# A decode step with grouped attention: VectorE's program as a loop, and the folding of the V groups moved to TensorE

## The chip, the core and the metric

One core of a Trainium2 chip runs the whole program. Its engines are TensorE (PE in the profile, its weight loads PEld), VectorE (DVE), ScalarE (ACT), GpSimd (POOL) and SyncE (SP), which here issues nearly all loads. Data comes from HBM into the on-chip SBUF; TensorE writes to PSUM, eight banks of 128 x 512 float32. The metric is the device time of one execution in microseconds (us), as the median of the runs.

## The reference

For a batch of 8 rows with 512 features, one decode step is computed, all in float32:

```python
xn = layernorm(x)
q = (xn @ wq) -> 32 heads of 128;  k, v: cached, 8 heads of 4096 x 128 (4 query heads share one)
scores = q . k * 128 ** -0.5
s = concat(softmax(scores) . v) @ wo
z = gelu(xn @ w_in)                       # 2 x 896
g = silu((z1 * (w_sp * layernorm(z2) + b_sp)) @ w_out)
return x + s * g
```

The caches of k and v hold 2 x 8 x 8 x 4096 x 128 numbers, 268 MB; wq and wo 8.4 MB each; the weights of the MLP 5.5 MB.

## The kernel before, in words

Three slots A, B and C of 8.4 MB in SBUF take every load. For each of the 8 key heads, four loads come in this order: K of batches 0 to 3 into A, K of batches 4 to 7 into B, V of batches 0 to 3 into C, V of batches 4 to 7 into B. At the start wq goes into B and the MLP's weights into C. In the last head V of batches 0 to 3 goes into A, the last V comes in two halves, and wo comes into C in seven pieces (`load_wo`). A load is queued on SP as soon as the last reader of its slot is done; the loads share one queue and are served in order.

TensorE's work for a head: `scores` (L506) multiplies the spread queries `qz` with K, in four column groups, so that the 4096 keys stand as 4 groups of 1024 in `sc`. `softmax` takes the maximum of each group (L510), exponentials (L511), the common maximum and sum over the groups by small transpositions and a product with `same`, a matrix of ones where two partitions belong together; it scales p (L524), turns it by eight transpositions (L528) and copies it to `tbuf` (L529). `values(b)` (L538) multiplies p of one batch with V in four column groups c: 16 rows of each group's 32 partitions of `o_ps` hold group x query row, 4 x 4, by 4 x 128 columns, of which only the blocks on the diagonal (group of the row equal to group of the columns) are wanted. VectorE masks the others away with `diag` (L540) and adds the four column blocks (L541) into `o_sb`. `combine(b)` (L544), issued behind the values of the next batch, then adds the four partition groups with one product of `o_sb` (128 x 128) by `fold` (128 x 4) into `po`. At the end of a head VectorE stores `po` into `oT` (L606), and spreads the next head's queries into `qz` (L499).

wo's products follow in the last head: `folded_wo` (L566) for the heads that are done, placed between and behind the last values, then `direct_wo` (L574) for the last two heads, a product that joins both (L625), and on VectorE the gate (L630) and the residual (L631).

The order is what the program's text gives. A recorder collects all operations with what they read and write and inserts the waits. TensorE runs the first seven heads as a hardware loop (`LOOPED = 7`), whose waits take tokens: the producer adds one, TensorE takes one. The last head and all other engines are written out.

Of the kernel before, what the change touches and what calls it, by code (L numbers as in the profile page):

```python
# [15 lines left out]
P = 128  # L16
# [3 lines left out]
G = 4  # L20
# [59 lines left out]
class Op:  # L80
    def __init__(self, eng, name, args, kw, line):
        self.eng, self.name, self.args, self.kw, self.line = eng, name, args, kw, line
        self.reads, self.writes = [], []
        self.waits = []
        self.sem = None
        self.iter = None
        self.pos = None


class Recorder:  # L90
# [6 lines left out]
    NAMES = ["tensor", "vector", "scalar", "gpsimd", "sync"]  # L97

    def __init__(self, nc):
        self.nc = nc  # L100
        self.ops = []
        self.touched = {}
        self.now = None
        self.rounds = 0
        self.order = {n: [] for n in self.NAMES}
        self.dma_sems = {}
        for n in self.NAMES:
            setattr(self, n, Proxy(self, n))

    @contextmanager  # L110
    def round(self, i):
        self.now = i
        self.rounds = max(self.rounds, i + 1)
        self.count = {n: 0 for n in self.NAMES}
        yield
        self.now = None

    def add(self, eng, name, args, kw):
# [3 lines left out]
        key = kw.pop("key", None)  # L122
# [15 lines left out]
        if self.now is not None:  # L138
            op.iter, op.pos = self.now, self.count[eng]
            self.count[eng] += 1  # L140
        op.at = len(self.order[eng])
# [3 lines left out]
        op.deps = set()  # L145
# [25 lines left out]
    def plan(self):  # L171
# [18 lines left out]
        body = [op for op in self.order["tensor"] if op.iter is not None]  # L190
        size = len(body) // self.rounds
        rounds = [body[i * size:(i + 1) * size] for i in range(self.rounds)]
        place = {(o.eng, o.iter, o.pos): o for o in self.ops if o.iter is not None}
        for p in range(size):
            need = set()
            for i, ops in enumerate(rounds):
                assert ops[p].pos == p and ops[p].name == ops[0 * size + p].name
                for o in ops[p].waits:
                    assert o.iter == i, (ops[p].line, ops[p].name, i, o.eng, o.line, o.iter)
                    need.add((o.eng, o.pos))  # L200
            for i, ops in enumerate(rounds):
                ops[p].waits = [place[e, i, q] for e, q in sorted(need)]
        takes = [o.pos for op in rounds[0] for o in op.waits if not o.dma]
        assert takes == sorted(set(takes)), takes
        assert all(o.dma or o.eng == "vector" for op in rounds[0] for o in op.waits)

        for op in self.ops:
            op.token = op.counted = False
        for op in self.ops:
            for o in op.waits:  # L210
                if o.dma:
                    continue
                if op.eng == "tensor" and op.iter is not None:
                    o.token = True
                else:
                    o.counted = True
        for p in range(size):
            any_ = any(ops[p].counted for ops in rounds)
            for ops in rounds:
                ops[p].counted = any_  # L220

        nc = self.nc
        self.first = None
        self.sems = {}

        def sem(name):
            if name not in self.sems:
                self.sems[name] = nc.alloc_semaphore(name)
            return self.sems[name]

        for n in self.NAMES:
            c = 0
            for op in self.order[n]:
                if op.dma:
                    op.sem = sem(op.key or f"dma{op.n}")
                    op.taken = op.key is not None
                    continue
                if op.token and op.counted:
                    c += 1
                elif op.counted:  # L240
                    c += 1
                op.level = c
            sem(n)
        sem("token")

    def emit_op(self, op):
        nc = self.nc
        eng = getattr(nc, op.eng)
        with nc.source_location(__file__, op.line, op.name):
            waits = []  # L250
            for o in sorted(op.waits, key=lambda o: o.n):
                if o.dma:
# [3 lines left out]
                    else:  # L256
                        waits.append((o.sem, 16))
                elif op.eng == "tensor" and op.iter is not None:
                    t = self.sems["token"]
                    eng.wait_ge(t, 1).then_inc(t, -1)  # L260
                else:
                    waits.append((self.sems[o.eng], o.level))
            for s, v in waits:
# [6 lines left out]
            elif op.counted:  # L270
                ins.then_inc(self.sems[op.eng], 1)
                if op.token:
                    eng.wait_ge(self.sems[op.eng], op.level).then_inc(self.sems["token"], 1)
            elif op.token:
                ins.then_inc(self.sems["token"], 1)

    def emit(self):
        nc = self.nc
        self.plan()
        for n in self.NAMES[1:]:  # L280
            for op in self.order[n]:
                self.emit_op(op)
        ops = self.order["tensor"]
        inside = [i for i, op in enumerate(ops) if op.iter is not None]
        size = len(inside) // self.rounds
        for op in ops[:inside[0]]:
            self.emit_op(op)
        with nc.tensor.Fori(0, self.rounds):
            for op in ops[inside[0]:inside[0] + size]:
                self.emit_op(op)  # L290
        for op in ops[inside[-1] + 1:]:
# [28 lines left out]
def gqa_gmlp_decode(real, x, kT, v, wq, wo, w_mlp, out):  # L320
# [13 lines left out]
    for c in range(0, XW, XW // X_PARTS):  # L334
# [22 lines left out]
    nc.vector.tensor_reduce(same[:, 0, :], ident.rearrange("p (g r) -> p r g", g=G),  # L357
                            op=ALU.add, axis=AX.X)
    for g in range(1, G):
        nc.vector.tensor_copy(same[:, g, :], same[:, 0, :])  # L360
# [5 lines left out]
    nc.vector.tensor_reduce(fold, same[:, 0, :G * REP].rearrange("p (g r) -> p r g", g=G),  # L366
                            op=ALU.add, axis=AX.X)
    same8 = sb("same8", [P, (E - 1) * B + R])
    nc.gpsimd.memset(same8, 0.0)
    nc.vector.tensor_copy(same8[:, (E - 1) * B:E * B], same[:, 0, :B])  # L370
# [8 lines left out]
    o_ps = [psum(f"o_ps{i}", [P, G, DH]) for i in range(2)]  # L379
    po = psum("po", [P, 512])[:, :B * REP]  # L380
    scr = [psum(f"scr{i}", [P, 512]) for i in range(3)]
    for t in o_ps:
        nc.vector.memset(t, 0.0)
# [5 lines left out]
    nc.vector.tensor_scalar(rstd[:, 0:1], mv[:, 1:2], EPS, None, op0=ALU.add)  # L389
# [5 lines left out]
    nc.vector.tensor_copy(xnT[:, :, :B], pt.rearrange("p (k b) -> p k b", k=NK))  # L395

    gate, xg, wb = sb("gate", [P, W]), sb("xg", [P, W]), sb("wb", [P, 2])
# [7 lines left out]
    nc.vector.tensor_copy(xg, px[:, :W])  # L405
    nc.vector.tensor_copy(wb, px[:, W:])
# [3 lines left out]
    def project_q(quad):  # L410
# [9 lines left out]
        tv = tq.rearrange("p (r g c) -> p r g c", r=REP, g=G)  # L420
        for g in range(G):
            h = quad * G + g
            nc.vector.tensor_copy(qT[:, h], tv[:, :, g, :B].rearrange("p r b -> p b r"))

    def mlp():
# [4 lines left out]
        pz = scr[1]  # L430
        nc.vector.memset(pz, 0.0)
# [9 lines left out]
        nc.vector.tensor_copy(zf, pz)  # L441
# [7 lines left out]
        def mean(src, pm, name):  # L449
# [3 lines left out]
            nc.vector.tensor_scalar(t, pm, 1.0 / FH, None, op0=ALU.mult)  # L453
# [6 lines left out]
        nc.vector.memset(u[(G - 1) * R:, 0, FH - (G - 1) * FQ:], 0.0)  # L460
        var = mean(u[:, 0, :], scr[2][:, :1], "var")
        nc.vector.tensor_scalar(var, var, EPS, None, op0=ALU.add)
# [8 lines left out]
        nc.vector.tensor_copy(hT.rearrange("p a s -> p (a s)"), th)  # L471
# [4 lines left out]
        nc.vector.tensor_copy(y_sb, sc[:, 0, :])  # L476
# [13 lines left out]
    nmin, full = sb("nmin", [1, R]), sb("full", [1, G, R])  # L490
    w, wl = sb("w", [P, 1]), sb("wl", [P, 1])
    oT = sb("oT", [P, FOLDED // REP, REP, B])
    o_all = [sb(f"o_all{i}", [P, G, DH]) for i in range(2)]
    o_sb = [sb(f"o_sb{i}", [P, DH]) for i in range(2)]
# [3 lines left out]
    def spread_q(h):  # L498
        nc.vector.tensor_copy(qz.rearrange("p (b s) -> p b s", b=B)[:, :, :REP], qT[:, h])  # L499
# [9 lines left out]
    def softmax():  # L509
        nc.vector.tensor_reduce(nm, sc, op=ALU.max, axis=AX.XY, negate=True)  # L510
        nc.scalar.activation(p.rearrange("p j s -> p (j s)"), sc.rearrange("p c s -> p (c s)"), AF.Exp,  # L511
                             bias=nm, accum_out=l)
        a, mm, tot = scr[0][:1, :P], scr[1][:, :1], scr[2][:, :1]
        nc.tensor.transpose(a, nm, ident)  # L514
        nc.vector.tensor_reduce(nmin, a.rearrange("b (g r) -> b r g", g=G), op=ALU.min, axis=AX.X)
        nc.vector.tensor_copy(full, nmin[:, None, :].to_broadcast([1, G, R]))
# [6 lines left out]
        nc.vector.tensor_mul(w, w, wl)  # L523
        nc.vector.tensor_scalar(p, p, w, None, op0=ALU.mult)  # L524
        for c in range(2):
            t = scr[c]
            for j in range(4):
                nc.tensor.transpose(t[:, j * P:(j + 1) * P], p[:, 4 * c + j, :], ident)  # L528
            nc.vector.tensor_copy(  # L529
                pT[:, :, 4 * c:4 * c + 4].rearrange("p b j (g r) -> p (j g) b r", g=G),  # L530
                t.rearrange("p (m b r) -> p m b r", b=B, r=REP))
# [133 lines left out]
```

## Time and profile before

| | |
|---|---|
| median of 3 runs | 678.88 us (678.7 to 678.92) |
| the profiled execution's span, first to last instruction | 677.3 us; its time outside the span is not listed, and the median stands 1.6 us above |
| TensorE busy | 375.2 us (55%), 2658 matmul passes |
| VectorE busy | 167.5 us (25%), 277 instructions |
| ScalarE, GpSimd busy | 13.4 us, 2.8 us |
| mean granted TensorE clock | 0.758 |
| read from HBM | 290.74 MB, 429 GB/s over the span |

A busy share is a mean over all stages, so it says little of what sets the end; for that, the stages of the loads and the tail are looked at one by one. A row of a timeline has the start, the time from the first start to the last end, engine, line and operation, output and inputs, and how many instructions were merged; in brackets the engine's idle time before it and what ended it. A float32 product shows as two passes. A row of the windows has the stretch, its length, each engine's busy time with its instructions, the granted TensorE clock, the share of time in which the DMA engines were busy, and GB/s. A row of a group has busy time and mean ns of one, then the engine's idle time ahead of the group and what ended it. A row of one line's durations has minimum, median and maximum in ns.

### The profile page before, as it was taken

To read this page: it belongs to the slowest core of one execution; us is meant where nothing else is said; L and a number is where in the kernel's file an instruction comes from. 1 tells how busy PE (TensorE), PEld (TensorE's weight loads), DVE (VectorE), ACT (ScalarE), POOL (GpSimd) and SP (SyncE) were. 2 spreads that over 40 slices of the span, in tenths; PEclk is the share of its full clock that TensorE was granted. 3 is DMA by queue.
4 is the path that set the end of the run, shared out by engine and by line. 5 is a ranking of instruction groups with operands and counts; after the bars stand their busy time and mean duration, and the time that the engine had idled before them with its cause. 6 is when DMAs were issued, how large, how long until landed. Compare 5 with 4: busy or idle time off the path is not lost. (4 is left out here: it accounts for less than half of the span.)

```text
span 677.3 us, 5857 instructions
## 1 busy us (share of the span) xinstructions
PE 375.2 (55%) x2658; PEld 119.5 (18%) x2658; DVE 167.5 (25%) x277; ACT 13.4 (2%) x27; POOL 2.8 (0%) x14
## 2 busy tenths in 40 slices
PE   0547554546665455456755454655654465655657
PEld 0122121112111111111211121211211121111212
DVE  2141042302430033401521024401432024400342
ACT  0000000000000000000000000000000000000000
POOL 1000000000000000000000000000000000000000
PEclk9967666878767678877766678887676678766697
DMA  8999999999999999999999999999999999999997
GB/s 373 449 434 434 433 434 433 434 433 433 433 433 433 433 433 433 434 433 433 433 433 433 433 434 433 433 433 437 437 437 437 433 437 445 433 437 434 404 423 318
DMA packets 6233, 290.90 MB, mean 429 GB/s; under 512 B 832, under 2 KB 848, under 8 KB 1360
## 3 DMA queue, kind: packets, MB, share of 16 engines
q1 hardware_dynamic: 6192, 290.75, 99.3%
q8 instruction: 7, 0.11, 0.1%
q10 hardware_dynamic: 32, 0.02, 0.0%
q14 instruction: 2, 0.02, 0.0%
HBM read 290.74 MB, written 0.03 MB: 429 GB/s over the span
## 5 line engine op out<-in xcount | busy, mean ns | idle before, releaser
L506 PE MATMUL sc<-slot_B,qz 128*32 128x512 f32 x512 | 74.4, 746 | 76.6 <-PEq L506 76.6
L538 PE MATMUL o_ps<-slot_B,tbuf 128*16 128x512 f32 x512 | 77.5, 732 | 70.5 <-PEq L538 61.6
L506 PE MATMUL sc<-slot_A,qz 128*32 128x512 f32 x512 | 74.4, 746 | 47.6 <-PEq L506 47.6
L540 DVE TENSOR_TENSOR o_all<-o_ps,diag 128x512 f32<-128x512 f32 x64 | 44.3, 691 | 161.0 <-PE o_ps L538 161.0
L538 PE MATMUL o_ps<-slot_C,tbuf 128*16 128x512 f32 x448 | 67.0, 739 | 20.5 <-PEq L538 20.5
L510 DVE TENSOR_REDUCE nm<-sc 128x1 f32<-128x1024 f32 x8 | 9.8, 1224 | 269.5 <-PE sc L506 269.5
L541 DVE TENSOR_REDUCE o_sb<-o_all 128x128 f32<-128x512 f32 x64 | 67.8, 1060 | 2.2
L506 PEld LDWEIGHTS sc<-slot_B,qz 128*32 128x32 f32 x512 | 20.4, 134 | 130.5 <-issue 130.5
L506 PEld LDWEIGHTS sc<-slot_A,qz 128*32 128x32 f32 x512 | 20.7, 133 | 94.8 <-issue 94.8
L544 PE MATMUL po<-fold,o_sb 128*128 128x4 f32 x128 | 25.6, 270 | 12.3 <-PEq L544 12.3
L544 PEld LDWEIGHTS po<-fold,o_sb 128*128 128x128 f32 x128 | 20.3, 199 | 68.5 <-issue 64.2
L538 PEld LDWEIGHTS o_ps<-slot_B,tbuf 128*16 128x16 f32 x512 | 13.4, 106 | 100.5 <-issue 90.2
L538 PEld LDWEIGHTS o_ps<-slot_C,tbuf 128*16 128x16 f32 x448 | 13.7, 112 | 57.0 <-issue 56.8
L528 PE MATMUL scr<-ident,pbuf 128*128 128x128 f32 x64 | 14.8, 409 | 10.6 <-PEq L528 9.3
L511 ACT ACTIVATE pbuf<-sc,nm 128x1024 f32<-128x1024 f32 x8 | 8.9, 1114 | 556.1 <-DVE nm L510 556.1
L528 PEld LDWEIGHTS scr<-ident,pbuf 128*128 128x128 f32 x64 | 11.8, 211 | 11.0 <-issue 9.7
L529 DVE COPY tbuf<-scr 128x512 f32<-128x512 f32 x16 | 11.1, 692 | 10.6 <-PE scr L528 10.6
L415 PE MATMUL scr<-slot_B,xnT 128*32 128x512 f32 x64 | 9.0, 713 | 8.2 <-PEq L415 8.2
L538 PE MATMUL o_ps<-slot_A,tbuf 128*16 128x512 f32 x64 | 9.8, 753 | 3.9 <-PEq L538 3.9
L514 PE MATMUL scr<-ident,nm 128*1 128x128 f32 x8 | 2.2, 269 | 11.8 <-PEq L514 10.4
L394 PE MATMUL scr<-ident,tbuf 8*128 8x8 f32 x4 | 0.6, 255 | 12.9 <-DVE tbuf L391 12.9
L521 PE MATMUL scr<-wl,same 128*128 128x1 f32 x16 | 3.5, 286 | 6.1 <-PEq L521 5.4
(102 smaller groups left out, 88.4 us busy)
## 6 DMA issues: line engine op xcount, KB each, us to landing
slot_B<-in_v SPq DMA_DIRECT2D x2, 4096.0 KB, 33.8
slot_C<-in_w_mlp SPq DMA_DIRECT2D x1, 5376.0 KB, 34.2
slot_C<-in_wo SPq DMA_DIRECT2D x1, 3072.0 KB, 35.4
slot_C<-in_wo SPq DMA_DIRECT2D x1, 2048.0 KB, 41.4
slot_C<-in_wo SPq DMA_DIRECT2D x1, 1280.0 KB, 44.0
slot_C<-in_wo SPq DMA_DIRECT2D x1, 768.0 KB, 45.4
slot_C<-in_wo SPq DMA_DIRECT2D x1, 512.0 KB, 46.1
slot_C<-in_wo SPq DMA_DIRECT2D x2, 256.0 KB, 46.4
```

Source lines behind the costliest of these rows:

```text
L415: nc.tensor.matmul(pq[R * g:R * (g + 1), :], xnT[:, k, :], wq_sb[:, k, lo:lo + REP * DH], start=(k == 0), stop=(k == NK - 1))
L506: nc.tensor.matmul(sc[R * g:R * (g + 1), c, :], qz[:, b * R:(b + 1) * R], k_sb[:, i, c, g, :], start=(b == 0), stop=(b == B - 1))
L510: nc.vector.tensor_reduce(nm, sc, op=ALU.max, axis=AX.XY, negate=True)
L511: nc.scalar.activation(p.rearrange("p j s -> p (j s)"), sc.rearrange("p c s -> p (c s)"), AF.Exp, bias=nm, accum_out=l)
L514: nc.tensor.transpose(a, nm, ident)
L521: nc.tensor.matmul(tot, same_all, wl, start=True, stop=True)
L528: nc.tensor.transpose(t[:, j * P:(j + 1) * P], p[:, 4 * c + j, :], ident)
L529: nc.vector.tensor_copy(pT[:, :, 4 * c:4 * c + 4].rearrange("p b j (g r) -> p (j g) b r", g=G), t.rearrange("p (m b r) -> p m b r", b=B, r ...
L538: nc.tensor.matmul(of[R * c:R * c + G * REP, :], pT[:, b, j, :], v_unit[:, j], start=(j < G), stop=(j >= J - G))
L540: nc.vector.tensor_mul(o_all[b % 2], o, diag[:, :, None].to_broadcast([P, G, DH]))
L541: nc.vector.tensor_reduce(o_sb[b % 2], o_all[b % 2].rearrange("p g d -> p d g"), op=ALU.add, axis=AX.X)
L544: nc.tensor.matmul(po[:, b * REP:(b + 1) * REP], o_sb[b % 2], fold, start=True, stop=True)
```

## The change

VectorE's program becomes a loop over the 8 heads with an inner loop of four turns, each of two batches. For that, all turns must have the same instructions: what differs from head to head or batch to batch by an address leaves VectorE. The store of `po` (its target changes with the head) goes to ScalarE, the spread of the queries (its source changes) to GpSimd, where it waits for that store. The mask and the reduction of each batch are gone: VectorE copies `o_ps` out as it is (`o_cp`), and `combine` is four products, one for each column block, whose 128 x 4 right sides (`fold`, now a view of `same`) choose the wanted rows and add the groups in PSUM. In the softmax, one reduction writes all four copies of the common maximum (`full`), one operation scales by `w` and `wl`, and the eight transpositions go to `sc` and are copied out at once; the exponential waits for the transposition of the maxima. In the preamble, copies go to ScalarE and small masks to GpSimd. The recorder gets tokens for both looping engines. The loads, their order and their slots are as before.

```diff
-    diag = sb("diag", [P, G])
-    nc.vector.tensor_reduce(diag, same[:, 0, :G * REP].rearrange("p (g r) -> p g r", g=G),
-                            op=ALU.add, axis=AX.X)
-    fold = sb("fold", [P, REP])
-    nc.vector.tensor_reduce(fold, same[:, 0, :G * REP].rearrange("p (g r) -> p r g", g=G),
-                            op=ALU.add, axis=AX.X)
+    fold = same[:, 0, :G * REP].rearrange("p (g r) -> p g r", g=G)
...
-        nc.vector.tensor_scalar(q_sb, pq, float(DH) ** -0.5, None, op0=ALU.mult)
+        nc.scalar.activation(q_sb, pq, AF.Copy, scale=float(DH) ** -0.5)
...
     def spread_q(h):
-        nc.vector.tensor_copy(qz.rearrange("p (b s) -> p b s", b=B)[:, :, :REP], qT[:, h])
+        nc.gpsimd.tensor_copy(qz.rearrange("p (b s) -> p b s", b=B)[:, :, :REP], qT[:, h], after=nc.stored)
...
         nc.vector.tensor_reduce(nm, sc, op=ALU.max, axis=AX.XY, negate=True)
+        a, mm, tot = scr[0][:1, :P], scr[1][:, :1], scr[2][:, :1]
+        turned = nc.tensor.transpose(a, nm, ident)
         nc.scalar.activation(p.rearrange("p j s -> p (j s)"), sc.rearrange("p c s -> p (c s)"), AF.Exp,
-                             bias=nm, accum_out=l)
...
+                             bias=nm, accum_out=l, after=turned)
+        nc.vector.tensor_reduce(full, a.rearrange("b (g r) -> b r g", g=G)[:, None].to_broadcast([1, G, R, G]),
+                                op=ALU.min, axis=AX.X)
...
-        nc.vector.tensor_mul(w, w, wl)
-        nc.vector.tensor_scalar(p, p, w, None, op0=ALU.mult)
...
+        nc.vector.tensor_scalar(p, p, w, wl, op0=ALU.mult, op1=ALU.mult)
+        t = sc.rearrange("p c s -> p (c s)")
+        for j in range(J):
+            nc.tensor.transpose(t[:, j * P:(j + 1) * P], p[:, j, :], ident)
+        nc.vector.tensor_copy(pT.rearrange("p b j (g r) -> p (j g) b r", g=G),
+                              t.rearrange("p (m b r) -> p m b r", b=B, r=REP))
...
-        nc.vector.tensor_mul(o_all[b % 2], o, diag[:, :, None].to_broadcast([P, G, DH]))
-        nc.vector.tensor_reduce(o_sb[b % 2], o_all[b % 2].rearrange("p g d -> p d g"), op=ALU.add, axis=AX.X)
+        with nc.turn(b // 2, b % 2):
+            nc.vector.tensor_copy(o_cp[b % 2], o)
 
     def combine(b):
-        nc.tensor.matmul(po[:, b * REP:(b + 1) * REP], o_sb[b % 2], fold, start=True, stop=True)
+        for g in range(G):
+            nc.tensor.matmul(po[:, b * REP:(b + 1) * REP], o_cp[b % 2][:, g, :], fold[:, g, :],
+                             start=(g == 0), stop=(g == G - 1))
...
-        nc.vector.tensor_copy(to, po.rearrange("p (b r) -> p r b", r=REP))
+        nc.stored = nc.scalar.activation(to, po.rearrange("p (b r) -> p r b", r=REP), AF.Copy)
```

How the instructions stand on TensorE at the end of the last head, before the change, from the values of the batch before last on (16x512 values, 128x4 products, then wo):

```order
L538 MATMUL o_ps<-slot_B,tbuf 16x512 x8
L544 MATMUL po<-fold,o_sb 128x4
L538 MATMUL o_ps<-slot_B,tbuf 16x512 x8
L544 MATMUL po<-fold,o_sb 128x4
L566 MATMUL sc<-slot_C,oT 8x512 x8
L544 MATMUL po<-fold,o_sb 128x4
L566 MATMUL sc<-slot_C,oT 8x512 x4
```

And after the change (`ob` is the PSUM tensor that holds `o_ps` and `po`):

```order
L594 MATMUL ob<-slot_B,tbuf 16x512 x8
L601 MATMUL ob<-same,o_cp 128x4 x4
L594 MATMUL ob<-slot_B,tbuf 16x512 x8
L601 MATMUL ob<-same,o_cp 128x4 x4
L624 MATMUL sc<-slot_C,oT 8x512 x8
L601 MATMUL ob<-same,o_cp 128x4 x4
L624 MATMUL sc<-slot_C,oT 8x512 x4
```

The places are the same; each of the three products became four in a row.

VectorE's part of a head, before, from the scaling of p through the first two batches:

```order
L524 TENSOR_SCALAR pbuf<-pbuf,w 128x1024
L529 COPY tbuf<-scr 128x16x8x4 x2
L540 TENSOR_TENSOR o_all<-o_ps,diag 128x512
L541 TENSOR_REDUCE o_sb<-o_all 128x128
L540 TENSOR_TENSOR o_all<-o_ps,diag 128x512
L541 TENSOR_REDUCE o_sb<-o_all 128x128
```

After, with the inner loop's start and end and the outer loop's end:

```order
L582 TENSOR_SCALAR pbuf<-pbuf,w,wl 128x1024
L586 COPY tbuf<-sc 128x32x8x4
L343 UNCONDITIONAL_BRANCH
L597 COPY o_cp<-ob 128x512 x2
L343 REGISTER_ALU
L343 COMPARE_AND_BRANCH
L340 REGISTER_ALU
L340 COMPARE_AND_BRANCH
```

Two operations a batch became one, and what was written out eight times stands once, between branches; the store of `po` and the spread of the queries, which followed here, stand on ScalarE and GpSimd.

More of the change, by code (lines that the diff above doesn't have):

```diff
@@ L144, in add @@
         self.ops.append(op)
-        op.deps = set()
+        if self.now is not None and not op.dma:
+            self.heads.setdefault(self.now, []).append(op)
+        op.deps = set() if after is None else {after}
         for regs, write in ((op.reads, False), (op.writes, True)):
@@ L283, in emit @@
+        with nc.vector.Fori(0, HKV):
+            for op in first:
+                if op is turn[0]:
+                    with nc.vector.Fori(0, count):
+                        for q in turn:
+                            self.emit_op(q)
+                elif op.turn is None:
+                    self.emit_op(op)
+        for op in ops[inside[-1].at + 1:]:
+            self.emit_op(op)
         ops = self.order["tensor"]
-        inside = [i for i, op in enumerate(ops) if op.iter is not None]
@@ L292, in emit @@
+        for op in ops[inside[-1].at + 1:]:
             self.emit_op(op)
```

252 lines of the change are left out of this document (145 added, 107 removed).

## The prediction

> **What bounds the kernel now.** I read the page's first parts, then the chain that ended last, then the queue's own waits, and only then single stretches of the timeline.
>
> ```profile
> PE 375.2 (55%) x2658; PEld 119.5 (18%) x2658; DVE 167.5 (25%) x277; ACT 13.4 (2%) x27; POOL 2.8 (0%) x14
> ...
> q8 instruction: 7, 0.11, 0.1%
> ...
> HBM read 290.74 MB, written 0.03 MB: 429 GB/s over the span
> ```
>
> No engine is busy for more than 55% of the span, but HBM delivers 429 GB/s from end to end. The same is seen stretch by stretch, and at the end of the chain (start us, us, what):
>
> ```profile
> 60.00:674.70 614.70, 351.23 (x2448) 109.70 (x2440) 150.75 (x224) 11.26 (x24) 0.00 (x0) 0.75 1.00 432
> ...
> 628.26 46.46 DMA slot_C<-in_wo
> ```
>
> From 60 to 674.7 us the DMA share is 1.00: one stream of loads without a hole. It ends when the last piece of wo lands at 628.26 + 46.46 = 674.72; what stands behind it is one step of the output projection (0.43, in the timeline below), two small VectorE operations, and the store. So the change can matter in two places only: where it makes the stream run dry, and in TensorE's work between the start of the last values (662.49) and the last piece of wo (674.72).
>
> The span is 677.3; the runs' median 678.88 lies 1.6 above it. I sum against the span and add the difference to the median.
>
> **VectorE's part.** Its work per batch shrinks:
>
> ```profile
> L541 DVE TENSOR_REDUCE o_sb<-o_all 128x128 f32<-128x512 f32 x64 | 67.8, 1060 | 2.2
> L540 DVE TENSOR_TENSOR o_all<-o_ps,diag 128x512 f32<-128x512 f32 x64 | 44.3, 691 | 161.0 <-PE o_ps L538 161.0
> L529 DVE COPY tbuf<-scr 128x512 f32<-128x512 f32 x16 | 11.1, 692 | 10.6 <-PE scr L528 10.6
> ```
>
> Mask (691 ns) and reduction (1060 ns) become one copy of 512 elements, 692 ns by the row of L529: 64 x 1.06 = 68 us of busy time less. None of it is on the path: VectorE waits for TensorE before 161 us of L540, and each batch's products come behind the next batch's values anyway. I cost it at 0. The loop adds branches. TensorE's own loop shows their price, 208 ns for one:
>
> ```profile
> L288 PEldq COMPARE_BRANCH  x7: 76/208/228, 126.6 to 590.6; - x7
> ```
>
> A turn lies between an odd batch's copy and the next even batch's; the next values take 1.84 us (rows below), the copy 0.7, so 0.2 fits, and 1 us would. Not below 0, since nothing waits there now. The shorter softmax (one operation fewer in two places, but one copy of 1024 behind all eight transposes) lies ahead of V's landing: 0. The exponential there now waits for TensorE's transposition of the maxima too; behind it on ScalarE stands only the exponential of w, which needs VectorE's later result anyway: 0.
>
> **The copies on ScalarE, the spread of q and the masks on GpSimd.** The preamble's lie under the first loads: a load that waits there for TensorE's reads of wq or of the MLP's weights is queued behind another that is still in flight. I cost them at 0; a late one would show as a hole in the stream's first 60 us. In a head, ScalarE now stores po and GpSimd spreads q, one behind the other, where VectorE did both:
>
> ```profile
> L499 DVE COPY qz<-qT 128x32 f32<-128x32 f32 x8 | 1.4, 171 | 0.0
> L464 POOL TENSOR_TENSOR rs<-var,neg_half 128x1 f32<-128x1 f32 x1 | 0.6, 569 | 37.4 <-DVE var L462 37.4
> L606 DVE COPY oT<-po 128x32 f32<-128x32 f32 x6 | 1.1, 192 | 3.2 <-PE po L544 3.2
> ```
>
> VectorE took 0.19 + 0.17 us. GpSimd's nearest row is an operation of 0.57 us, so I take 1.2 us for both with their hand-overs, at most 2, at least VectorE's own 0.4. Scores of the next head wait for it; whether K has landed by then is the next part. On SP, no load waits for either copy.
>
> **The fold on TensorE.** This is the term that counts: each batch has four products of 128x128 by 128x4 instead of one, 192 more. A product is two passes:
>
> ```profile
> L544 PEld LDWEIGHTS po<-fold,o_sb x128: 186/189/338, 100.2 to 671.3; 128*128 128x128 f32 x128
> L544 PE MATMUL po<-fold,o_sb x128: 244/253/377, 100.3 to 671.4; 128*128 128x4 f32 x128
> ...
> 671.23 0.30 PEld L544 LDWEIGHTS po<-fold,o_sb 128*128 128x128 f32 x2 [0.86 <-DVE o_sb L541]
> ```
>
> And in TensorE's timeline of the tail (idle before in brackets):
>
> ```profile
> 652.80 1.91 PE L538 MATMUL o_ps<-slot_B,tbuf 128*16 128x512 f32 x16 [3.59 <-DMA slot_B<-in_v]
> 654.64 0.38 PE L544 MATMUL po<-fold,o_sb 128*128 128x4 f32 x2
> 654.96 1.91 PE L538 MATMUL o_ps<-slot_B,tbuf 128*16 128x512 f32 x16
> 656.80 0.38 PE L544 MATMUL po<-fold,o_sb 128*128 128x4 f32 x2
> ...
> 662.49 3.61 PE L538 MATMUL o_ps<-slot_B,tbuf 128*16 128x512 f32 x16 [5.30 <-DMA slot_B<-in_v]
> 666.03 0.59 PE L544 MATMUL po<-fold,o_sb 128*128 128x4 f32 x2
> 666.55 2.61 PE L538 MATMUL o_ps<-slot_B,tbuf 128*16 128x512 f32 x16
> 669.09 0.39 PE L544 MATMUL po<-fold,o_sb 128*128 128x4 f32 x2
> 669.40 1.90 PE L566 MATMUL sc<-slot_C,oT 128*8 128x512 f32 x16
> 671.23 0.38 PE L544 MATMUL po<-fold,o_sb 128*128 128x4 f32 x2
> 671.55 1.04 PE L566 MATMUL sc<-slot_C,oT 128*8 128x512 f32 x8
> 672.41 1.52 PE L574 MATMUL sc<-slot_C,oT_end 128*32 128x64 f32 x80
> 673.75 0.41 PE L625 MATMUL sc<-pbuf,same 128*32 128x64 f32 x16
> 673.97 0.63 PE L574 MATMUL sc<-slot_C,oT_end 128*32 128x64 f32 x32
> 674.76 0.43 PE L574 MATMUL sc<-slot_C,oT_end 128*32 128x64 f32 x16 [0.16 <-DMA slot_C<-in_wo]
> ```
>
> A lone product holds TensorE for 0.32 us (654.64 to 654.96). Three more in a row cost between the pitch of weight loads (0.30 - 0.19 = 0.11 a pass, 0.66 a batch) and three times the lone one (0.96). The matmuls' pitch is 0.38 - 0.25 = 0.13, so I take 0.7 a batch, near the lower end, 1.02 for the four; at half clock 0.59 - 0.38 = 0.21 a pass, some 1.3 more, at most 3 x 0.52 = 1.56.
>
> *Between heads* it is covered. The closest call is the load of the next head's second K half, issued when slot B has been read:
>
> ```profile
> 434.59 0.33 SPq L547 DMA_DIRECT2D slot_B<-in_kT  x1
> ...
> 434.46 0.39 PE L544 MATMUL po<-fold,o_sb 128*128 128x4 f32 x2
> ...
> 442.85 3.53 PE L506 MATMUL sc<-slot_A,qz 128*32 128x512 f32 x16 [6.00 <-PEq L506]
> ```
>
> The load ahead of it lands by 442.85, 8.2 us later. Three batches' products stand ahead of that issue: 3 x 0.7 and some 0.6 for one at half clock, 2.7 us; the load is then queued 5.5 us before the stream needs it. The two last batches' products and the spread of q put the next scores some 3 us behind that, still ahead of 442.85. Cost 0; if the cover were gone, each us over would be paid in seven heads.
>
> *In the tail* there is nothing after it to hide under. At full clock, from V's landing: values 1.84 (652.80 to 654.64), products 1.02, values 1.84, products 1.02, wo 1.83 (669.40 to 671.23), products 1.02, wo 0.86 (671.55 to 672.41): 662.49 + 9.43 = 671.92, where before stood 672.41. The rest, by its rows, takes 1.34 + 0.22 + 0.63 + 0.43 = 2.62: 674.5. The last wo piece forces 674.76 + 0.43 = 675.19 in any case. So at full clock the three times 0.7 are hidden: 0. But before, the same stretch lost 2.6 us at half clock (values 3.54 and 2.54 instead of 1.84, a product 0.52 instead of 0.32), and nobody noticed, because it ended at the landing. What counts is thus how long the clock is halved. Stretches of 3.41 us (PE busy, then granted clock):
>
> ```profile
> 295.95:299.37 3.42, 1.38 (x16) 1.00 0.80 345
> 299.37:302.78 3.41, 0.00 (x0) 0.50 1.06 461
> ...
> 650.94:654.35 3.41, 1.55 (x16) 1.00 1.02 442
> ...
> 657.77:661.18 3.41, 0.00 (x0) 1.00 0.97 418
> 661.18:664.59 3.41, 2.10 (x12) 0.50 0.99 423
> 664.59:668.00 3.41, 3.41 (x18) 0.50 0.95 405
> 668.00:671.42 3.42, 3.42 (x32) 1.00 0.99 414
> ```
>
> The clock changes at the bounds of these stretches: it is halved after one that was 40% busy (1.38), kept after 45% (1.55), not restored after 62% (2.10), restored after 100%. In the changed kernel the first V quarter takes until 652.80 + 2 x 2.86 = 658.52, so TensorE idles 3.97 us before 662.49, not 5.3. Some stretch then has over 1.95 us of idleness in it, so the clock is halved, but for how long hangs on where the bounds fall, which I take as equally likely anywhere. With 80% taken as what restores it, in six positions of ten it is one stretch of working time (2.6 to 3.4 us), in nearly four (a bound 1.95 to 3.2 us into the idleness) 4.8 to 6.1. The loss is 2.6/5.5 = 0.47 a us: 1.6 at most, or 2.6. From 674.5: 676.1, or 677.1; against 675.19 that is +0.9, or +1.9. **The sum: +0.9 us**, span 678.2, median 679.8.
>
> By the Trainium skill ("TensorE: Matmul & The Clock Gate", Part 1) the clock falls to half only after at least one idle window of about 3.4 us, free-running against the program. By that rule 3.97 us of idleness would hold a whole window in one position of six, the tail would run at full clock, and the median would be 678.9; the row at 295.95 speaks against it, since 40% busy was not enough, so I give it the smaller chance below.
>
> **The rivals.**
> - *Two halved stretches, or dearer products: slower.* The tail loses 2.6, or a product more costs 0.32 as a lone one does (three batches, +0.8): 680.6 to 681.5, say 680.8. It decides once the halved clock lasts over 4.3 us of working time. For it: before, 662.49 to 668.00 was halved for 5.5 us. Against it: the shorter idleness.
> - *Wholly hidden:* the clock stays up, or the passes overlap at 0.11: 678.9.
> - *The stream runs dry between heads: slower.* It would need the load at 434.59 to be some 6 us later, twice my 2.7; 0.3 us in seven heads is 681. The stream's share of 1.00 at each head speaks against it.
> - *Faster:* VectorE's 277 instructions become a loop, and fewer instruction fetches share the engines with the stream. They are seven packets on q8 and 0.1% of 16 engines; the slowest engine sets each landing, so as much as 1 to 1.5 us could be given back: 677.6.
>
> **How the numbers follow.** One halved stretch 0.48, the slower tail 0.30, hidden 0.12, a dry stream 0.05, faster 0.05. The likeliest gives 679.8 (its own range 679.3 to 680.4). The range runs from just under the old time to the slow tail with the upper price: 678.5 to 681.5. A change of 0.2% is 1.36 us, about what can be told from none. Within it lie the hidden case and most of the first (0.42): 0.54; slower is the slow tail, the dry stream and the rest of the first (0.06): 0.41; faster 0.05.
>
> **What would show it.** In the profile after: DMA share 1.00 to about 674.7 as before, and wo's last landing there; L597's copy near 0.69 us x64; four products in 1.02 us at full clock; the next head's K issued some 2.7 us later than now; the mean granted clock above 0.758, since idle gaps shrink. In the tail, the last product ends behind the landing of wo by more than 0.47 us, with TensorE busy from 662.5 without a break. The forecast is wrong if TensorE waits for wo at the end (hidden), if the DMA share drops between heads, or if VectorE's copy comes late behind a turn of its loop, so that L601 waits for it.

## The result and the profile after

| | before | after |
|---|---|---|
| median | 678.73 us (678.47 to 679.05, 14 runs) | 681.74 us (679.61 to 687.01, 14 runs) |
| ratio to before | | 1.0046, 95% interval 1.0034 to 1.0059 |
| span of the profiled execution | 677.3 us | 680.4 us (its time 681.95) |
| mean granted TensorE clock | 0.758 | 0.772 |

The change makes the kernel slower by 3.1 us (2.3 to 4.0): beyond 0.2%, and above the upper end of the predicted range. The runs also spread over 7 us where those of before lie within 0.6.

The page of the changed kernel, the rows that answer to those of before (busy time of the engines, the copy and the fold):

```profile
PE 419.6 (62%) x3042; PEld 165.2 (24%) x3042; DVE 91.5 (13%) x147; ACT 18.2 (3%) x42; POOL 6.0 (1%) x29
...
L597 DVE COPY o_cp<-ob 128x512 f32<-128x512 f32 x64 | 44.2, 691 | 232.4 <-DVEq L597 232.4
...
L601 PE MATMUL ob<-same,o_cp 128*128 128x4 f32 x512 | 70.5, 263 | 4.5 <-PEq L601 4.5
```

VectorE has 76 us of busy time less and TensorE 44 more; neither says anything of the end. The end is read from the chain of work that ended last (start us, us, what):

```profile
625.59 37.86 DMA slot_B<-in_v
663.45 0.04 issue
663.49 2.83 PE ob L594 x16
666.32 1.80 PE ob L601 x8
668.12 3.36 PE ob L594 x16
671.49 0.99 PE ob L601 x8
672.47 1.83 PE sc L624 x16
674.30 0.98 PE ob L601 x8
...
677.60 0.71 PE sc L632 x48
```

Before, the last link from memory was the last piece of wo, and TensorE waited for it. Now it is the last V, and from there TensorE works without a break to 678.31; wo is no link of the chain any more. So the 3.1 us have two parts. The last values start at 663.49 instead of 662.49: +1.0, a loss in the stream of loads. From there to the end of the span the kernel takes 16.9 us (680.4 - 663.49) instead of 14.8 (677.3 - 662.49): +2.1, a loss in the tail.

In the tail the size of the fold is as forecast: four products took 0.98 to 0.99 us at full clock and 1.80 halved, against 1.02 and some 1.8 (0.5 + 1.3). What lasted longer is the half clock, as the windows of TensorE there show (stretch, length, PE busy and instructions, granted clock, DMA share, GB/s):

```profile
657.52:660.94 3.42, 3.42 (x31) 1.00 0.98 422
660.94:664.35 3.41, 1.12 (x11) 1.00 0.95 408
664.35:667.76 3.41, 3.41 (x19) 0.50 0.99 417
667.76:671.17 3.41, 3.41 (x18) 0.50 0.98 407
671.17:674.59 3.42, 3.42 (x31) 1.00 0.70 279
```

The stretch from 664.35 is busy from end to end, and still the next one is halved too. It holds values until 666.32 (1.97 us, 58%) and then folds (the chain above). The next is nearly all values (3.05 of 3.41 us from 668.12 on), and behind it the clock is back. TensorE thus worked at half clock for 6.8 us. Worth in the chain: values 2.83 and 3.36 instead of 1.84, a fold 1.80 instead of 0.98, together 3.3 us over full clock.

The same mechanism stands between the heads, where the load of the next head's second K half is issued behind the last values (TensorE, SP, ScalarE and GpSimd in the timeline of the changed kernel):

```profile
423.29 3.62 PE L594 MATMUL ob<-slot_B,tbuf 128*16 128x512 f32 x16 [6.91 <-PEq L594]
...
428.63 3.62 PE L594 MATMUL ob<-slot_B,tbuf 128*16 128x512 f32 x16
...
438.25 0.33 SPq L605 DMA_DIRECT2D slot_B<-in_kT  x1
438.58 1.92 PE L601 MATMUL ob<-same,o_cp 128*128 128x4 f32 x16 [0.67 <-PEq L601]
440.54 0.20 ACT L666 ACTIVATE oT<-ob 128x32 f32<-128x32 f32 x1 [43.51 <-PE ob L601]
440.79 0.21 POOL L558 COPY qz<-qT 128x32 f32<-128x32 f32 x1 [78.97 <-ACT oT L666]
442.66 4.79 PE L565 MATMUL sc<-slot_A,qz 128*32 128x512 f32 x28 [2.17 <-PEq L565]
```

The load was issued at 434.59 before and at 438.25 now. From the landing times in the traces (each of the 16 DMA engines reports the end of its share of a load): the first of the 16 is done with the load ahead at 440.6 before and at 440.9 now, while the last of them is done by 442.66. So the next load came 6.1 us ahead of the first engine's end before, and 2.6 us now. Over all seven heads these margins are 6.1 to 7.4 us before and 2.6 to 5.4 now.

### The profile page after: what moved, and what is told of

Its sections match the earlier page's. It is cut to its first block, busy times and chain, and to the rows that moved or that the text cites. A ratio compares the mean times of both kernels' runs of the same rounds, so it can differ in the third digit from the quotient of the medians.

```text
span 680.4 us, 6804 instructions
## 1 busy us (share of the span) xinstructions
PE 419.6 (62%) x3042; PEld 165.2 (24%) x3042; DVE 91.5 (13%) x147; ACT 18.2 (3%) x42; POOL 6.0 (1%) x29
## 5 line engine op out<-in xcount | busy, mean ns | idle before, releaser
L594 PE MATMUL ob<-slot_B,tbuf 128*16 128x512 f32 x512 | 81.4, 766 | 53.9 <-PEq L594 48.8
L601 PEld LDWEIGHTS ob<-same,o_cp 128*128 128x128 f32 x512 | 65.8, 202 | 63.5 <-issue 63.5
L597 DVE COPY o_cp<-ob 128x512 f32<-128x512 f32 x64 | 44.2, 691 | 232.4 <-DVEq L597 232.4
L594 PE MATMUL ob<-slot_C,tbuf 128*16 128x512 f32 x448 | 65.9, 729 | 15.2 <-PEq L594 15.2
L601 PE MATMUL ob<-same,o_cp 128*128 128x4 f32 x512 | 70.5, 263 | 4.5 <-PEq L601 4.5
L594 PEld LDWEIGHTS ob<-slot_B,tbuf 128*16 128x16 f32 x512 | 13.8, 108 | 84.1 <-issue 77.6
L594 PEld LDWEIGHTS ob<-slot_C,tbuf 128*16 128x16 f32 x448 | 13.5, 111 | 51.1 <-issue 50.8
L585 PE MATMUL sc<-ident,pbuf 128*128 128x128 f32 x64 | 15.5, 423 | 11.4 <-PEq L585 11.4
L585 PEld LDWEIGHTS sc<-ident,pbuf 128*128 128x128 f32 x64 | 12.5, 223 | 11.9 <-issue 11.9
L586 DVE COPY tbuf<-sc 128x1024 f32<-128x1024 f32 x8 | 9.8, 1224 | 17.9 <-DVEq L586 17.9
```

The source lines that it names most:

```text
L585: nc.tensor.transpose(t[:, j * P:(j + 1) * P], p[:, j, :], ident)
L586: nc.vector.tensor_copy(pT.rearrange("p b j (g r) -> p (j g) b r", g=G), t.rearrange("p (m b r) -> p m b r", b=B, r=REP))
L594: nc.tensor.matmul(of[R * c:R * c + G * REP, :], pT[:, b, j, :], v_unit[:, j], start=(j < G), stop=(j >= J - G))
L597: nc.vector.tensor_copy(o_cp[b % 2], o)
L601: nc.tensor.matmul(po[:, b * REP:(b + 1) * REP], o_cp[b % 2][:, g, :], fold[:, g, :], start=(g == 0), stop=(g == G - 1))
```

## Experiments

Three theories stand after the result. *Tail* (T): the longer half clock in the tail is the loss; that the fold's products are no work for the clock is its later form (N). *Dry stream* (D): the loads issued later are it. *Loop* (L): VectorE's loop and the moved copies are it. Each run below is compared with runs of the kernel before on the same chip (medians 678.56 to 678.79).

### The fold on TensorE in one stage alone

The kernel before, with the plain copy and four products in the last head alone (tail_only), or in all heads but the last (loop_only, the condition turned round); the rest stays on VectorE:

```diff
-        nc.vector.tensor_mul(o_all[b % 2], o, diag[:, :, None].to_broadcast([P, G, DH]))
-        nc.vector.tensor_reduce(o_sb[b % 2], o_all[b % 2].rearrange("p g d -> p d g"), op=ALU.add, axis=AX.X)
...
+        if h == HKV - 1:
+            nc.vector.tensor_copy(o_all[b % 2], o)
+        else:
+            nc.vector.tensor_mul(o_all[b % 2], o, diag[:, :, None].to_broadcast([P, G, DH]))
+            nc.vector.tensor_reduce(o_sb[b % 2], o_all[b % 2].rearrange("p g d -> p d g"), op=ALU.add, axis=AX.X)
...
+        if h == HKV - 1:
+            for g in range(1 * G):
+                nc.tensor.matmul(po[:, b * REP:(b + 1) * REP], o_all[b % 2][:, g % G, :], fold4[:, g % G, :],
+                                 start=(g % G == 0), stop=(g % G == G - 1))
+        else:
+            nc.tensor.matmul(po[:, b * REP:(b + 1) * REP], o_sb[b % 2], fold, start=True, stop=True)
```

> The kernel before, with the four products and the plain copy in the last head alone (VectorE's mask and reduction stay in heads 0 to 6, nothing loops on VectorE). Theory T (the time is lost in the tail, by three times three more products and a longer half clock): as long as the changed kernel, 680.0 to 682 against 678.7, with a spread of 2 us or more between runs. Rival D (the stream runs dry between the heads): 678.7, since heads 0 to 6 are as before. Rival L (VectorE's loop, ScalarE's and GpSimd's copies cost): 678.7.

> The kernel before, with the four products and the plain copy in heads 0 to 6 alone. T: 678.7, within 0.3, runs as close together as before. D: over 680, and the far runs of the changed kernel (683, 687) show here. L: 678.7.

Measured: tail_only 680.58 us (679.2 to 682.12, 6 runs), ratio 1.0034 (1.0021 to 1.0047), +2.3 us. loop_only 679.01 us (678.52 to 681.94, 12 runs), ratio 1.0012 (1.0003 to 1.0020), +0.8 us. The two make 3.1 together, what the whole change costs; with intervals this wide, and since after_warm and warm_heads below don't add up so, that is in part luck. The six runs of tail_only fall into two groups, 679.2 to 679.7 and 681.5 to 682.1. The profiled one, 679.39, is of the cheap group; TensorE's windows in its tail:

```profile
662.05:665.46 3.41, 3.00 (x16) 0.50 0.99 425
665.46:668.87 3.41, 3.41 (x31) 1.00 0.99 420
```

Here the bounds lie so that the halved stretch holds values alone (16 instructions, no fold; 88% busy), and it is over after one. TensorE ends 13.3 us after the last V's landing (662.46 to 675.74), against 14.8 in the changed kernel. Same code in the tail, another position of the windows.

In loop_only's profile, of a run of 680.21 us and so 1.2 above its median, the loads were issued later (434.59 became 438.47), and wo, which landed at 674.72 before, landed at 676.22:

```profile
438.47 0.33 SPq L557 DMA_DIRECT2D slot_B<-in_kT  x1
```

```profile
628.68 47.54 DMA slot_C<-in_wo
...
676.26 0.47 PE sc L584 x16
```

T had forecast 678.7 with close runs for loop_only, D over 680 there and 678.7 for tail_only; none of these came. So T and D each hold a part (together they are theory S below): the larger in the tail, the rest between the heads.

### The loop with the fold left on VectorE, and the fold without the loop

after_vecfold is the changed kernel whose turn masks and reduces on VectorE again; both_unrolled is the kernel before with the plain copy and four products in all heads, everything else as it was:

```diff
...
         with nc.turn(b // 2, b % 2):
-            nc.vector.tensor_copy(o_cp[b % 2], o)
+            nc.vector.tensor_mul(o_cp[b % 2], o, diag[:, :, None].to_broadcast([P, G, DH]))
+            nc.vector.tensor_reduce(o_sb[b % 2], o_cp[b % 2].rearrange("p g d -> p d g"), op=ALU.add, axis=AX.X)
...
-        for g in range(G):
-            nc.tensor.matmul(po[:, b * REP:(b + 1) * REP], o_cp[b % 2][:, g, :], fold[:, g, :],
-                             start=(g == 0), stop=(g == G - 1))
+        nc.tensor.matmul(po[:, b * REP:(b + 1) * REP], o_sb[b % 2], fold, start=True, stop=True)
```

> The changed kernel with mask and reduction back on VectorE, inside its loop's turns, and one product a batch: the loop and all copies on ScalarE and GpSimd stay. T and D: 678.7, within 0.3. L: 680 or more.

> The kernel before with the four products and the plain copy in all eight heads, VectorE written out and the copies where they were. S: as the changed kernel, 680.5 to 682.5 with far runs, since the loop and the copies on ScalarE and GpSimd cost nothing. Rival L (part of the loss is the loop's, by its hand-overs): clearly under the changed kernel's 681.7, at 680 or less.

Measured: after_vecfold 678.94 us (678.61 to 679.09, 11 runs), ratio 1.0005 (0.9996 to 1.0014). Its chain ends as before, at wo's landing:

```profile
628.06 46.44 DMA slot_C<-in_wo
...
674.54 0.47 PE sc L637 x16
```

both_unrolled 681.53 us (681.26 to 681.8, 5 runs), ratio 1.0043 (1.0030 to 1.0056). Its chain's last part:

```profile
625.58 36.67 DMA slot_B<-in_v
...
662.30 3.61 PE o_ps L538 x16
665.91 1.80 PE po L551 x8
667.71 3.55 PE o_ps L538 x16
671.25 1.22 PE po L551 x8
```

The loop, the copies on ScalarE and GpSimd and the shorter softmax, taken together, cost nothing that can be told (+0.3 us, within -0.3 and +1.0); the fold alone gives the whole slowdown. In both_unrolled's profile the last V even landed 0.2 us earlier than before, and both values and one fold ran halved: the tail alone filled the 3.1 us of its span (680.4). The far runs that S had forecast for it did not come in its five (681.26 to 681.8).

### Products of 4 columns and products of 288 columns

Is it the number of columns? The kernel before, with 24 products added in each head behind the first half of the scores, where TensorE has time. Their results are read by nobody. burst_narrow has the shape of the fold, burst_wide the same count of products and weights with 288 columns:

```diff
+            if half == 0:
+                for _ in range(24):
+                    nc.tensor.matmul(scr[2][:, :REP], ident, fold, start=True, stop=True)
```

```diff
+            if half == 0:
+                for _ in range(24):
+                    nc.tensor.matmul(scr[2][:, :B * (R + REP)], ident, qz, start=True, stop=True)
```

> The kernel before with a burst of 24 idle products of 128x128 weights by 4 columns behind each head's first scores, where TensorE waits 9 us for K. Theory N (products of few columns keep TensorE busy in the records but are not work to what sets the clock): the clock, full at the end of the scores, is halved within the burst although TensorE is over 90% busy. Rival B (any busy time counts): full clock through the whole burst.

> As the burst of narrow products, with the same weights and 288 columns instead of 4. N and B: the clock stays full through the whole burst, and the second scores start at full clock where less than 2 us of idleness are left.

Both ran as long as before, 678.83 and 678.85 us (one run each). One narrow burst in TensorE's timeline, and its windows:

```profile
375.06 7.93 PE L585 MATMUL scr<-fold,ident 128*128 128x4 f32 x48
```

```profile
374.39:377.81 3.42, 3.42 (x33) 1.00 0.93 402
377.81:381.22 3.41, 3.41 (x18) 0.50 1.02 442
381.22:384.63 3.41, 1.87 (x13) 0.50 0.93 404
```

The stretch from 374.39 is wholly busy and 80% narrow products (from 375.06 on): behind it the clock is halved. The one from 377.81 is wholly busy with narrow products alone: the clock isn't restored. The wide burst in the same place of the same head:

```profile
373.33:376.75 3.42, 3.42 (x25) 1.00 0.84 364
376.75:380.16 3.41, 3.41 (x16) 1.00 0.84 365
380.16:383.57 3.41, 3.41 (x16) 1.00 1.20 519
```

Just as busy, and never halved. The other seven heads of both profiles show the same: the clock is halved at the latest as each narrow burst ends, and in no wide one. So a stretch can be full of 4-column products by the records and all but idle for the clock. How little they count can be estimated: in the first head's narrow burst the stretch from 67.20 to 70.61 was wholly busy, 33% with scores and 67% with narrow products, and the clock was halved behind it, where 45% of wide products alone kept it in the kernel before (650.94). If scores and values count alike, narrow products count for less than (0.45 - 0.33) / 0.67, under a fifth of their time.

### Keeping the clock up

Products of 512 columns whose results nobody reads are put into TensorE's idle time: in the tail alone (after_warm), in the first seven heads alone (warm_heads), in both (after_warm_loop), all on the changed kernel:

```diff
...
+    def warm(n):
+        for _ in range(n):
+            nc.tensor.matmul(scr[2][:R, :], ident[:, :R], tbuf[:, :512], start=True, stop=True)
...
+                    warm(4)
...
+                if not last and b == HALF - 1:
+                    warm(10)
+                if last and b == HALF + 1:
+                    with nc.apart():
+                        warm(4)
```

after_warm has the calls with 4 and multiplies a piece of slot A; warm_heads has the call with 10.

> The changed kernel with four idle products of 512 columns each (32 columns of weights, results unused) in TensorE's two waits for the last two loads of V, 1.7 us each at full clock, so that the clock is not halved. T: most of the loss goes: 678.9 to 680, TensorE at full clock from the last landing of V on, and what is left is a later landing. D and L: as the changed kernel, about 681.5.

> The changed kernel with the ten idle wide products a head in heads 0 to 6 alone, none in the tail. Theory S (two separate losses): the loads come as before the change (wo at 674.7), and the tail alone costs what it costs in the kernel with the four products in the last head alone, 680.0 to 681 with a spread of 2 us or more. Rival J (the tail's loss is only the late landings of V and wo): 678.9, close together.

> The changed kernel with idle wide products in every wait of TensorE for the second V half (ten of 512 columns, 4.3 us at full clock, in heads 0 to 6; four in each of the tail's two waits), so that values and folds run at full clock. Theory S (two losses: the loads of the next head's second K half are queued less than 3 us ahead of need and the stream thins there, and the tail runs at half clock): the issue is some 3 us earlier again, over 4.5 us ahead of the landing in all heads; wo lands at 674.7 again; 678.6 to 679.2. Rival F (the landings are late for another reason, such as instruction fetches that meet on one DMA engine): wo still lands 1 us or more late, 679.7 or more.

Measured: after_warm 681.32 us (679.82 to 682.47, 6 runs), ratio 1.0035 (1.0023 to 1.0047); warm_heads 681.92 (678.65 to 684.81, 12 runs), 1.0041 (1.0026 to 1.0056); after_warm_loop 678.91 (678.58 to 679.24, 11 runs), 1.0003 (0.9994 to 1.0012). Each alone mends little, both together the whole. T had forecast 678.9 to 680 for after_warm, and S 680.0 to 681 for warm_heads; both came out dearer (warm_heads with three of its twelve runs at 678.65 to 678.93, the others at 681.65 and more). The losses that are left, 2.4 and 2.8 us, make more than the whole 3.1, so the two parts don't simply add.

In after_warm's profile, of the slowest of its six runs (682.47), the clock stays full in the tail from 642.24 on, but the stream is late: the last values start at 666.06 instead of 662.49, and the chain ends on wo's landing at 678.23.

```profile
129.41 0.33 SPq L605 DMA_DIRECT2D slot_B<-in_kT  x1
...
666.06 1.91 PE L594 MATMUL ob<-slot_B,tbuf 128*16 128x512 f32 x16 [0.55 <-DMA slot_B<-in_v]
```

```profile
630.31 47.92 DMA slot_C<-in_wo
...
678.27 0.47 PE sc L636 x16
```

The load at 129.41 was issued 2.6 us ahead of the first engine's end on the load before it, and all 16 engines' landings slipped by 0.8 us on the mean with it; two later ones, 2.6 and 2.0 us ahead, slipped by 0.2 and 0.3 more. That is more than in loop_only, which has the same folds between the heads (0.9 us of slip in all by its last load, against 1.7, of which 0.3 was there before the first fold), and the times differ as well (+2.4 and +0.8 us by the ratios, with runs that overlap). So loop_only's 0.8 us is no upper bound for the heads' part in the changed kernel; why the stream lost more here on the mean of the engines is open. In warm_heads every margin is 4.2 us or more and wo lands as before (674.6), so its loss is the tail's alone. Its windows there:

```profile
657.78:661.19 3.41, 0.68 (x7) 1.00 0.97 413
661.19:664.60 3.41, 2.20 (x12) 0.50 1.00 428
664.60:668.02 3.42, 3.42 (x20) 0.50 0.96 408
668.02:671.43 3.41, 3.41 (x17) 0.50 0.99 410
671.43:674.84 3.41, 3.41 (x30) 1.00 0.53 208
```

Three halved stretches, the middle one wholly busy, half of it values and half folds. In after_warm_loop, with both, TensorE runs through the tail at full clock and margins are 4.5 to 5.8 us:

```profile
652.00:662.30 10.30, 10.30 (x60) 1.00 0.96 410
662.30:674.50 12.20, 12.20 (x215) 1.00 0.89 371
```

The whole loss is gone though the fold still costs TensorE its 0.7 us more a batch. This mends the change; it isn't faster than the kernel before, which no version here beats.

### The dose between heads

loop_only with every sum made twice, eight products a batch:

```diff
-            for g in range(1 * G):
+            for g in range(2 * G):
                 nc.tensor.matmul(po[:, b * REP:(b + 1) * REP], o_all[b % 2][:, g % G, :], fold4[:, g % G, :],
                                  start=(g % G == 0), stop=(g % G == G - 1))
```

> The kernel before with eight products instead of four in heads 0 to 6 (each sum is made twice, the second time counts). S: the issue comes another 3 us later, after or within a us of the landing ahead of it; the stream runs dry for 1 to 3 us in most of the seven heads: 684 to 695. F: about as the four products, 679 to 680.

Measured: 711.51 us (703.01 to 721.09, 4 runs), ratio 1.053 (1.0464 to 1.0596). Two of its loads, and the windows ahead of them (stretch, length, granted clock, DMA share, GB/s):

```profile
294.64 0.33 SPq L557 DMA_DIRECT2D slot_B<-in_kT  x1
...
377.23 0.33 SPq L557 DMA_DIRECT2D slot_B<-in_kT  x1
```

```profile
287.00:296.00 9.00, 0.54 0.28 95
374.00:379.00 5.00, 1.00 0.57 197
```

The load at 294.64 came 7.4 us after the first engine had run dry, and 8.6 us of the stream were lost there. That is S's dry stream, but its size was missed: 711.5 against 684 to 695. Even in the profiled run, the fastest of the four, three heads lost 8.6, 5.3 and 8.4 us and the other four 0.1 to 0.8, where 1 to 3 in most heads had been forecast.

## Why the prediction was wrong

**What bounds.** The frame held: the runs show a loss where the stream thins and in the tail, and nowhere else. The shorter work of VectorE brought nothing (after_vecfold, both_unrolled).

**VectorE's part, the copies.** Cost 0, as forecast. The copy took 691 ns (692 forecast). A branch of VectorE's inner loop takes 50 to 63 ns, not TensorE's 208:

```profile
L343 DVEq COMPARE_BRANCH  x32: 50/56/63, 100.2 to 671.8; - x32
```

Store and spread took 0.20 and 0.21 us, with the hand-over 0.46 (440.54 to 441.00), where 1.2 was taken.

**The fold's products.** 1.02 us for four at full clock, 0.98 to 0.99 measured; at half clock 1.80 as forecast. The choice of the lower pitch over the lone product's 0.32 was right.

**In the tail: the failed step.** It is the length of the half clock, "one stretch of working time (2.6 to 3.4 us)", as the likeliest. I took the busy share of a stretch as what the clock goes by, and let 80% of it restore it, with the folds counted in. They count for little (under a fifth, by the burst). In the changed kernel the stretch from 664.35 was 100% busy and 58% values, under the 62% that the trace of before had shown not to be enough, so it was followed by another halved one: 6.8 us of working time, 3.3 us lost, where the forecast had 1.6 at most, and 2.6 in the slower tail. Taking 0.7 a batch for the fold and yet judging the clock by a share that those 0.7 raise is the error; had they been left out, a stretch with one batch's folds at half clock (1.8 of 3.41 us) could not have restored it. In the prediction's own sum TensorE ends at 676.1 (674.5 + 1.6); it ended at 678.3, 2.2 later: 1.7 for the half clock (3.3 instead of 1.6) and 1.0 for the later V, less 0.6 for a term that was too big. The 2.62 for the rest of the output projection were summed from rows with overlapping ends and a wait for wo; without a break the same products took 2.05 (676.26 to 678.31). The cheap case exists: tail_only's profiled execution is the likeliest of the forecast, its span 677.8 against the 678.2 of the sum. It comes when the bounds let a stretch hold values alone. The rival of two halved stretches had the right mechanism and 680.8, still 0.9 under the median. The longer cases show in other profiles too, 6.8 us of work in the changed kernel, and three halved stretches in warm_heads and both_unrolled.

By the rule of the Trainium skill ("TensorE: Matmul & The Clock Gate", Part 1) a whole idle window was needed to halve the clock. The trace disagrees again: 660.94 to 664.35 was 33% busy (1.12 of 3.41) and the next stretch was halved.

**Between heads: cost 0 was too little.** Two sizes were off. The issue moved by 3.7 us where I had 2.7: the folds took 2.6 of it, as forecast, but from 418.59 to 432.24 the clock was halved for 13.65 us, in the kernel before from 418.83 to 429.07, 10.24 (the same mechanism as in the tail). The second batch's values thus took 3.55 instead of 2.54, 1.0 more, which I had not counted. And I measured the room by the landing of the whole load ahead (442.85). The first of 16 engines is done some 2 us sooner, and the margin to that is the measure that I use now. Where it was under 3.2 us, the stream lost between 0 and 0.8 us at a load, and under 0.1 at eight of the fifteen; with 4 us or more, 0.1 at most (mean over the 16 engines, in all profiles of this study but loop_double's). I had asked for 6 us of delay; the loss begins at a delay of between 3 and 4. The rival, a dry stream with 0.3 us a head, was right in kind; it is not seven equal losses but unequal ones at some of the heads whose issue comes late, and loop_only puts their sum at 0.8 us (0.2 to 1.4), while after_warm, with the tail at full clock, still lost 2.4.

Late issues explain only a part of the later V. In the changed kernel's profile the engines' mean slip at the last loads is 0.3 to 0.4 us (burst_wide, whose loads were never late, shows 0.4 too), while the last V comes 1.0 later. That is the work of one engine. The program's instructions are fetched in packets of 16 KB (8 on q8 in the changed kernel) over the same 16 engines. In the kernel before, a fetch makes one engine some 1.4 us late: behind the fetch at 624.26 six engines land about 1.5 us after the others, behind the one at 656.64 seven, and the last landing stays where it was. In the changed kernel's profile the fetch at 644.63 took 0.89 us, and the next packet of 64 KB on its engine 1.76 instead of 1.21; that engine lands the first V quarter at 653.79, 1.1 behind the next one (652.67), and the last V at 663.45, again 1.1 behind (662.34). The engines that land last in loop_only (fetch at 620.50) and in after_warm (fetch at 662.95, the last V 2.2 us behind the next engine) had run a fetch as well. So a fetch moves the landing where it meets an engine that is not among the early ones. With margins of 4.2 us and more, the fetches did not make the last V late (after_warm_loop, warm_heads). That thin margins make such a meeting likelier is not shown: no run moved the fetches, and in both_unrolled, with margins down to 2.6, the fetch at 645.73 met an early engine and cost nothing.

It is not shown either why single runs reached 687.0 in the changed kernel and 684.8 in warm_heads: only one execution of each is profiled. A tail at half clock throughout is a guess.

**What would show it.** Most of the signs named came: the copy at 0.69 us, the fold near 1.02 (0.98), TensorE busy without a break to an end behind wo's landing. Two did not: wo's last landing came at 675.73 and not at 674.7, and the issue between heads 3.7 us later and not 2.7. The signs told the mechanism and not its size. The mean clock rose (0.758 to 0.772) while the loss came from a longer half clock in the one place that has no cover: as a sign it spoke for the change, and it was worth nothing.

## What to carry to other kernels

Before moving small work to TensorE because it has idle time, ask what the clock makes of it: a product of few columns takes time without keeping the clock up, and it dilutes the stretches that would restore it. Price such a tail by the share of wide products in a stretch, not by the busy share, and count the halved stretches again with the new work in. For a queue of loads like this one, measure the room from the issue to the first engine's end, and keep some 4 us of it.

## What the runs showed of the hardware

- 48 passes of 128 x 128 by 4 columns, 7.93 us long, let the clock fall to half behind a wholly busy stretch and kept it there; the same with 288 columns kept it at 1.00. The prediction had counted them as work.
- The clock was halved behind stretches 33% and 40% busy, and restored behind one that was 88% busy with values alone; 76% with values alone did not restore it (both_unrolled, 661.47 to 664.88), nor did 58% values with 42% folds.
- The 16 engines finish a load of 8.4 MB 1.7 to 2.1 us apart in the kernel before (4.1 for the last V in after_warm), and a load queued behind it can lose time, 0 to 0.8 us, once it is issued less than about 3 us ahead of the first of them.
- An instruction fetch of 16 KB (0.89 us) makes the engine that runs it some 1.4 us late for the loads behind it.
- A compare and branch of VectorE's loop took 56 ns, one of TensorE's 208 (medians).
